# Streaming attention heads in tiles of 55 queries with all their 118 keys, in place of 96-key tiles

## The chip, the cores and the metric

One core of a Trainium2 chip. The metric is the device time of one execution in microseconds (us). Times are medians of the fast runs. A run is called slow when it lies over 1.5% above the fastest of the same kernel; slow runs are not used. Ratios are the mean time of one kernel's fast runs over that of the kernel before in the same rounds, so they are not quite the ratio of the medians quoted beside them. In the profiles PE is TensorE, ACT ScalarE, DVE VectorE, POOL GpSimd and SP SyncE; `[0.73 <-ACT ...]` says how long an engine stood still and what, as far as the profile can tell, ended the wait. The granted clock is the share of full speed that TensorE was given. PSUM is the memory that the matmuls here write. The kernel uses it in banks, and a matmul into a bank is made to wait for the engine that still reads it (in the kernel before, 0.35 us for ACT at 156.24 us).

## The reference, cut to what matters

Four batches of 8 attention heads over 768 positions, head size 64, then a mixture of four experts over all 3,072 rows. Three heads (0, 2, 6) see all earlier keys. Five heads (1, 3, 4, 5, 7) are streaming heads: each query sees the first 4 keys (the sinks) and the last 64.

```python
is_sink = pos[None, :] < 4
in_win = (rel >= 0) & (rel < 64)
stream_keep = causal & (is_sink | in_win)
scores = np.where(mask, scale * (q @ k.T), -1e9)
a = softmax(scores)                      # per row, with 1e-9 in the denominator
x = (a @ v) as rows of 8 * 64 = 512 columns
out = sum over e of p[:, e] * (relu(x @ w1[e]) @ w2[e])   # 512 -> 1024 -> 512
```

## The kernel before

The work goes in eight groups of 384 positions: batch b, half c (0 or 1). While TensorE runs the experts of group g, the attention of group g + 1 is woven in between as small steps, and GpSimd loads k, q and v for group g + 2. From batch 1 on, q and k go through staging tiles in row layout and are transposed by DMA. Scores stand with keys on the partitions, so a matmul takes one tile of keys as weights and the queries as its moving columns. Cuts are marked with `...`.

```python
TK = 96; R0 = P - TK; TQ = TK + NW            # a key tile: 96 keys, seen by up to 160 queries
kSr = [pers.tile([P, TC, NSH, P], FP16, ...) for c in range(NCH)]   # staging, one per half

def tiles_of(x, b, h, c):                     # 96 partitions, 4 tiles, 64 elements
    return x[b, h, c*CH:(c+1)*CH, :].rearrange("(t r) d -> r t d", r=TK)

def load_k(b, c):                             # fp32 in HBM -> fp16 in SBUF, issued by GpSimd
    for h in range(H):
        ...
        gp.dma_start(out=kSr[c][R0:P, :, SH.index(h), own(h)], in_=tiles_of(k, b, h, c))

def score_tiles(h):                           # streaming head: (key tile, column, first query, queries)
    if c == 0: return [(320, [(0, 0, 0, 160), (1, 160, 96, 160)], mask),
                       (256, [(2, 0, 192, 160), (3, 160, 288, 96)], mask)]
    return [(384, [(3, 0, 0, 64), (4, 64, 0, 160), (5, 224, 96, 160)], mask),
            (256, [(6, 0, 192, 160), (7, 160, 288, 96)], mask)]

def scores(h):                                # per score tile: matmuls, exp, mask
    for cols, parts, masks in score_tiles(h):
        ps = bank()                           # 4 PSUM banks, shared with the experts' first layer
        for n, (t, o, q0, nq) in enumerate(parts):
            nc.tensor.matmul(out=ps[:, o:o+nq], lhsT=key_tile(b, h, t), rhs=qTs[b, c][:, hp, q0:q0+nq], ...)
            ns += mm_ns(nq)                   # PE time as the kernel counts it, nq / 2.4 + 2.5 ns (384: 162.5; step in the trace 162)
        es = ...; nc.scalar.activation(out=es, in_=ps, func=AF.Exp, scale=SC)
        ... multiply by the mask on VectorE ...
        yield ns                              # values(h) yields likewise, then Ln and Exp on ScalarE

att_ns = 4500.0 if nxt % NCH == 0 else 7700.0 # total of the attention's ns for a half
for ns in moe_group(g):                       # weave by PE time spent
    spent += ns
    while done < (spent - begin) / (end - begin) * att_ns: done += next(att_steps)
```

The softmax here doesn't subtract the row's maximum and nothing guards it: scores larger than these inputs give would overflow.

## Time and profile before

| | before |
|---|---|
| median of 3 runs | 417.87 us (417.56 to 418.0) |
| span in the profile | 415.6 us |
| TensorE (PE) busy | 401.6 us, 97% |
| granted clock | 0.996 (1.00 from 68 to 415 us) |
| GpSimd's queue q0 | 71,872 packets |

The prediction below shows the lines of busy time, chain, matmuls and stalls. The records of matmuls overlap: one of 384 columns is recorded with 326 ns, and the next one starts 162 ns after it. So PE's stream is counted in steps from start to start. Two more lines, both of the first page of the kernel before: the share of time in which the DMA engines were busy, a digit of tenths for each of 40 slices (10.4 us each), and the packets, megabytes and share of the 16 engines' time of the GpSimd queue q0.

```profile
DMA  9999999999994700069963600046001000020002
...
q0 software_dynamic: 71872, 17.05, 45.8%
```

The engines are full until 125 us and then have long empty stretches.

### The profile page before, as it was taken

The numbers are of one execution on the slowest core, as the hardware profiler recorded it, in microseconds if no ns is written. First come the engines' busy times: TensorE is split into PE (matmuls) and PEld (weight loads), VectorE is DVE, ScalarE is ACT, GpSimd is POOL, SyncE is SP. The second block draws the span as 40 slices with busy tenths as digits, with TensorE's granted clock in tenths as the row PEclk, the third lists the DMA queues.
The fourth block names the chain that finished last, engine by engine and source line by source line (L and its number), as shares of the span: only waits on it lengthen the run. The fifth ranks groups of instructions, "written<-read, shape, count | busy, mean of one in ns | idle before, by whom it ended". The sixth has DMA issues, their size and how long they took to land.

```text
span 415.6 us, 6541 instructions
## 1 busy us (share of the span) xinstructions
PE 401.6 (97%) x2520; PEld 228.3 (55%) x2520; DVE 163.3 (39%) x332; ACT 249.3 (60%) x539; POOL 120.2 (29%) x176
## 2 busy tenths in 40 slices
PE   7899999999999999999999999999999999999996
PEld 4665554555555555555555555555555555555552
DVE  7976553224432335333433333234443233432222
ACT  2676874337775657666764558666665577653331
POOL 8938319897980000039930000000000000000000
PEclk9899999999999999999999999999999999999999
DMA  9999999999994700069963600046001000020002
GB/s 173 146 196 204 209 205 109 177 182 146 88 91 118 98 1 2 25 126 164 83 39 94 117 2 2 0 107 105 2 0 61 18 2 0 2 76 2 0 0 76
DMA packets 117554, 33.70 MB, mean 81 GB/s; under 512 B 108100, under 2 KB 112404, under 8 KB 117524
## 3 DMA queue, kind: packets, MB, share of 16 engines
q0 software_dynamic: 71872, 17.05, 45.8%
q1 hardware_dynamic: 42452, 15.46, 18.1%
q10 hardware_dynamic: 3200, 0.79, 0.9%
q8 instruction: 19, 0.31, 0.3%
q14 instruction: 11, 0.09, 0.1%
HBM read 35.70 MB, written 6.29 MB: 101 GB/s over the span
## 4 chain that ended last, share of the span: by engine, by line
PE 86%; ACT 6%; DVE 4%; issue 1%; DMA 1%; ACTq 0%; DVEq 0%
PE pO L669 39%; PE pA L648 35%; PE pV L529 5%; PE pA L481 5%; ACT hs L661 2%; ACT rc L548 2%; DVE kS L417 1%; DMA q<-in_q_dram 1%; DVE vS L218 1%; ACT es L499 1%; ACT rc L558 1%; DVE kR L401 1%; ACTq L279 0%; DVE qT L392 0%; DVE es L503 0%
## 5 line engine op out<-in xcount | busy, mean ns | idle before, releaser
L648 PE MATMUL pA<-xT,w1sb 128*128 128x384 f16 x1024 | 187.7, 326 | 1.5 <-DVE kS L417 1.0
L669 PE MATMUL pO<-w2sb,hs 128*128 128x512 f16 x768 | 180.7, 379 | 0.0
L661 ACT ACTIVATE hs<-pA 128x384 f16<-128x384 f32 x256 | 121.3, 493 | 80.0 <-PE pA L648 73.4
L648 PEld LDWEIGHTS <-w1sb 128*128 128x128 f16 x1024 | 97.3, 98 | 59.7 <-issue 1.8
L669 PEld LDWEIGHTS <-hs 128*128 128x128 f16 x768 | 72.8, 98 | 72.7 <-ACT hs L661 0.5
L499 ACT ACTIVATE es<-pA 128x256 f16<-128x256 f32 (+3 forms) x152 | 71.6, 481 | 32.5 <-PE pA L481 29.5
L685 DVE SCALAR_TENSOR_TENSOR acc<-pO,p_sb,acc 128x512 f32<-128x512 f32 x72 | 54.0, 750 | 85.3 <-PE pO L669 84.8
L503 DVE TENSOR_TENSOR es<-es,mS 128x384 f16<-128x384 f16 (+1 forms) x70 | 22.2, 317 | 85.4 <-ACT es L499 85.0
L548 ACT ACTIVATE rc<-pV,eps 64x384 f32<-64x384 f32 x60 | 34.5, 575 | 34.7 <-PE pV L529 33.9
L173 POOL DMA_DIRECT2D kSr<-in_k_dram x30 | 20.9, 700 | 54.9 <-DMA kSr<-kSr 42.1
L553 DVE TENSOR_TENSOR xT<-pV,rc 64x384 f16<-64x384 f32 x60 | 33.1, 552 | 4.1 <-PE pA L648 1.7
L681 DVE TENSOR_SCALAR acc<-pO,p_sb 128x512 f32<-128x512 f32 x24 | 18.0, 750 | 37.7 <-PE pO L669 36.8
L558 ACT ACTIVATE rc<-rc 64x384 f32<-64x384 f32 x58 | 30.2, 522 | 1.8
L211 POOL DMA_DIRECT2D vS<-in_v_dram x40 | 28.1, 706 | 2.9 <-DMA q<-in_q_dram 2.2
L481 PE MATMUL pA<-qT,kS 128*128 128x160 f16 (+2 forms) x180 | 23.7, 223 | 3.4 <-ACT es L499 1.8
L481 PE MATMUL pA<-qT,kR 128*128 128x384 f16 (+2 forms) x120 | 25.3, 281 | 0.0
L481 PEld LDWEIGHTS <-kS 128*128 128x128 f16 x180 | 15.9, 98 | 15.2 <-issue 4.5
L503 DVE TENSOR_TENSOR es<-es,mC 128x256 f16<-128x256 f16 (+1 forms) x42 | 10.8, 256 | 29.4 <-ACT es L499 29.0
L529 PE MATMUL pV<-es,vR 128*128 128x384 f16 (+2 forms) x120 | 21.9, 281 | 0.0
L169 POOL DMA_DIRECT2D kRr<-in_k_dram x18 | 13.5, 751 | 21.4 <-issue 17.1
L207 POOL DMA_DIRECT2D vR<-in_v_dram x24 | 18.2, 759 | 4.5 <-DMA w2sb<-in_moe_w_dram 4.2
L529 PEld LDWEIGHTS <-vS 128*128 128x128 f16 x180 | 13.7, 98 | 9.8 <-issue 2.2
(68 smaller groups left out, 153.0 us busy)
## 6 DMA issues: line engine op xcount, KB each, us to landing
out_dram<-acc SPq DMA_DIRECT2D x24, 256.0 KB
w1sb<-in_moe_w_dram POOLq DMA_DIRECT2D x4, 1024.0 KB, 14.6
w2sb<-in_moe_w_dram POOLq DMA_DIRECT2D x4, 1024.0 KB, 17.6
q<-in_q_dram POOLq DMA_DIRECT2D x18, 128.0 KB, 4.8
vS<-in_v_dram POOLq DMA_DIRECT2D x40, 48.0 KB, 3.3
kSr<-in_k_dram POOLq DMA_DIRECT2D x30, 48.0 KB, 4.5
vR<-in_v_dram POOLq DMA_DIRECT2D x24, 48.0 KB, 3.4
kRr<-in_k_dram POOLq DMA_DIRECT2D x18, 48.0 KB, 4.6
```

The costliest lines, as they stand in the source:

```text
L211: gp.dma_start(out=t[R0:P, TC * c : TC * (c + 1), own(h)], in_=tiles_of(v, b, h, c),)
L481: nc.tensor.matmul(out=ps[:, o : o + nq], lhsT=key_tile(b, h, t), rhs=qTs[b, c][:, hp, q0 : q0 + nq], start=(n == 0 or not first), stop=no ...
L499: nc.scalar.activation(out=es[:, 0:cols], in_=ps[:, 0:cols], func=AF.Exp, scale=SC)
L503: nc.vector.tensor_tensor(out=es[:, o0:o1], in0=es[:, o0:o1], in1=m[:, mo : mo + o1 - o0], op=ALU.mult,)
L529: nc.tensor.matmul(out=ps[:, q0 : q0 + nq], lhsT=v_tile(b, h)[:, t, :], rhs=es[:, o : o + nq], start=(n == 0), stop=(n == len(work) - 1), ...
L548: nc.scalar.activation(out=rc[r, :], in_=ps[o, 0:CH], func=AF.Ln, bias=eps[o, :])
L553: nc.vector.tensor_tensor(out=xT[g][r, hp, :], in0=ps[r, 0:CH], in1=rc[r, :], op=ALU.mult)
L558: nc.scalar.activation(out=rc[r, :], in_=rc[r, :], func=AF.Exp, scale=-1.0)
L648: nc.tensor.matmul(out=pss[ft][:, 0:CH], lhsT=w1sb[:, e * DMP + ct, ft * P : (ft + 1) * P], rhs=xT[g][:, ct, :], start=(ct == 0), stop=(ct ...
L661: nc.scalar.activation(out=hs[:, ft, :], in_=ps[:, 0:CH], func=AF.Relu)
L669: nc.tensor.matmul(out=ps_o, lhsT=hs[:, ft, j * P : (j + 1) * P], rhs=w2sb[:, e * FTP + ft, :], start=(ft == 0), stop=(ft == FTP - 1),)
L685: nc.vector.scalar_tensor_tensor(out=acc[nt], in0=ps_o, scalar=p_ap, in1=acc[nt], op0=ALU.mult, op1=ALU.add,)
```

## The change

The intent: cut the columns that PE streams for the streaming heads. A tile of 96 keys is streamed past 160 queries, though each query sees only 68 keys, so many queries pass two tiles. After the change a tile is 55 queries with every key that any of them sees: 55 + 63 = 118 consecutive keys, plus the 4 sinks, 122 of 128 partitions. Each query is then streamed exactly once. The price is that neighbouring tiles' keys overlap, so rows are loaded more than once.

```diff
+    WQ = 55
+    WK = WQ + NW - 1                      # 118
+    WT = 7
-    kSr = [pers.tile([P, TC, NSH, P], FP16, name=f"kSr{c}") for c in range(NCH)]
+    kSr = pers.tile([P, WT, NSH, P], FP16, name="kSr")       # one staging tile (kRr likewise)
+    def windows_of(x, b, h, c):
+        first = ((b * H + h) * S + c * CH - NW) * D
+        return bass.AP(x.tensor, x.offset + first, [[D, WK], [WQ * D, WT], [1, D]])
     ... load_k, load_v, batches 1 to 3 ...
-                    out=kSr[c][R0:P, :, SH.index(h), own(h)], in_=tiles_of(k, b, h, c)
+                    out=kSr[NS : NS + WK, :, SH.index(h), own(h)],
+                    in_=windows_of(k, b, h, c),
     ... score_tiles ...
+            if b:
+                starts = [max(WQ * t - 1, 0) for t in range(WT)] + [CH]
+                parts = [(t, q0, q0, q1 - q0) for t, (q0, q1) in enumerate(zip(starts, starts[1:]))]
+                return [(CH, parts, [(mWf, 1 + 2 * WQ * c, 0, CH)])]
-        att_ns = 4500.0 if nxt % NCH == 0 else 7700.0
+        att_ns = 3700.0 if nxt % NCH == 0 else 6600.0
```

Left out: the new mask mW, the copies of the sinks, and the sharing of buffers between batches. Batch 0 keeps the old tiles.

More of the change, by code (lines that the diff above doesn't have):

```diff
@@ L67 @@
     assert NS <= R0 and NW == 64 and NS + NW <= TK
+    WQ = 55
+    WK = WQ + NW - 1
+    WT = 7
+    assert WT * WQ - 1 == CH and NS + WK <= P
     pers = ctx.enter_context(tc.tile_pool(name="pers", bufs=1))
@@ L89, with windows @@
     kR = []
-    kS = []
+    kSf = []
     vR = []
-    vS = []
+    vSf = []
     for i in range(2):
         kR.append(pers.tile([P, NCH, NR, 3, P], FP16, name=f"kR{i}"))
-        kS.append(pers.tile([P, NCH, TC, NSH, P], FP16, name=f"kS{i}"))
+        kSf.append(pers.tile([P, NCH * TC * NSH * P], FP16, name=f"kS{i}"))
         vR.append(pers.tile([P, S // P, len(RH), P], FP16, name=f"vR{i}"))
-        vS.append(pers.tile([P, NT, len(SH), P], FP16, name=f"vS{i}"))
+        vSf.append(pers.tile([P, NT * NSH * P], FP16, name=f"vS{i}"))
+    kS = kSf[0].rearrange("p (c t s x) -> p c t s x", c=NCH, t=TC, s=NSH)
+    vS = vSf[0].rearrange("p (t s x) -> p t s x", t=NT, s=NSH)
+    def windows(x, c):
+        return x[1 - c][:, 0 : WT * NSH * P].rearrange(
+            "p (t s x) -> p t s x", t=WT, s=NSH
+        )
     ident32 = pers.tile([P, P], FP32, name="ident32")
@@ L106 @@
     mS = pers.tile([P, 4, TQ], FP16, name="mS")
+    mW = pers.tile([P, WT + 2, WQ], FP16, name="mW")
     probs = pers.tile([P, NTILE, E], FP32, name="probs")
@@ L110 @@
     p_sb = pers.tile([P, NTILE, E], FP32, name="p_sb")
-    kRr = [pers.tile([P, NR, 3, P], FP16, name=f"kRr{c}") for c in range(NCH)]
-    kSr = [pers.tile([P, TC, NSH, P], FP16, name=f"kSr{c}") for c in range(NCH)]
+    kRr = pers.tile([P, NR, 3, P], FP16, name="kRr")
+    kSr = pers.tile([P, WT, NSH, P], FP16, name="kSr")
     def own(h):
@@ L119, in own, with key_tile @@
         return slice(u * D, (u + 1) * D)
-    def key_tile(b, h, t):
+    def key_tile(b, c, h, t):
         i = b % 2
@@ L125, in key_tile, with v_tile @@
             return kR[i][:, t // 3, RH.index(h), t % 3, :]
-        return kS[i][:, t // TC, t % TC, SH.index(h), :]
-    def v_tile(b, h):
+        if b:
+            return windows(kSf, c)[:, t, SH.index(h), :]
+        return kS[:, t // TC, t % TC, SH.index(h), :]
+    def v_tile(b, c, h):
         i = b % 2
@@ L132, in v_tile @@
             return vR[i][:, :, RH.index(h), :]
-        return vS[i][:, :, SH.index(h), :]
+        if b:
+            return windows(vSf, c)[:, :, SH.index(h), :]
+        return vS[:, :, SH.index(h), :]
     q16 = {}
@@ L142, in tiles_of @@
         return x[b, h, c * CH : (c + 1) * CH, :].rearrange("(t r) d -> r t d", r=TK)
+    def windows_of(x, b, h, c):
+        assert b > 0
+        first = ((b * H + h) * S + c * CH - NW) * D
+        return bass.AP(x.tensor, x.offset + first, [[D, WK], [WQ * D, WT], [1, D]])
     def load_by_rows(x, x16, b, c):
@@ L169, in load_k @@
                 gp.dma_start(
-                    out=kRr[c][:, RH.index(h), :, own(h)], in_=rows_of(k, b, h, c)
+                    out=kRr[:, RH.index(h), :, own(h)], in_=rows_of(k, b, h, c)
                 )
@@ L183, in dma_transposes @@
         i = b % 2
-        first = kSr[0][R0 : R0 + NS, 0:1, :, :].rearrange("p t s x -> p t (s x)")
-        nc.sync.dma_start(
-            out=kSr[c][0:NS, :, :, :].rearrange("p t s x -> p t (s x)"),
-            in_=first.to_broadcast([NS, TC, NSH * P]),
-        )
+        if c == 0:
+            x = kSr.rearrange("p t s x -> p t (s x)")
+            nc.sync.dma_start(
+                out=x[0:NS, :, :],
+                in_=x[NS + NW : 2 * NS + NW, 0:1, :].to_broadcast([NS, WT, NSH * P]),
+            )
         alloc_qT(b, c)
@@ L195, in dma_transposes @@
             )
-        for x, xr in ((kR, kRr), (kS, kSr)):
+        for x, xr in ((kR[i][:, c, :, :, :], kRr), (windows(kSf, c), kSr)):
             nc.sync.dma_start(
-                out=x[i][:, c, :, :, :].rearrange("p t s x -> p (t s) x"),
-                in_=xr[c].rearrange("p t s x -> p (t s x)"),
+                out=x.rearrange("p t s x -> p (t s) x"),
+                in_=xr.rearrange("p t s x -> p (t s x)"),
                 transpose=True,
@@ L204, in load_v @@
         for h in heads:
-            t = v_tile(b, h)
+            t = v_tile(b, c, h)
             if RETR[h]:
@@ L208, in load_v @@
                     out=t[:, 3 * c : 3 * c + 3, own(h)], in_=rows_of(v, b, h, c)
+                )
+            elif b:
+                gp.dma_start(
+                    out=t[NS : NS + WK, :, own(h)], in_=windows_of(v, b, h, c)
                 )
@@ L216, in sink_row @@
     def sink_row(b, h, c):
-        t = v_tile(b, h)[:, :, own(h)]
+        t = v_tile(b, c, h)[:, :, own(h)]
         nc.vector.tensor_copy(
@@ L223, in sink_rows @@
     def sink_rows(b, c):
-        x = vS[b % 2].rearrange("p t s x -> p t (s x)")
-        nc.sync.dma_start(
-            out=x[0:NS, TC * c : TC * (c + 1), :],
-            in_=x[R0 : R0 + NS, 0:1, :].to_broadcast([NS, TC, NSH * P]),
-        )
+        x = vS.rearrange("p t s x -> p t (s x)")
+        to, src = x[0:NS, TC * c : TC * (c + 1), :], x[R0 : R0 + NS, 0:1, :]
+        if b:
+            to, x = (
+                windows(vSf, y).rearrange("p t s x -> p t (s x)") for y in (c, 0)
+            )
+            to = to[0:NS, :, :]
+            src = x[0:NS, 0:1, :] if c else x[NS + NW : 2 * NS + NW, 0:1, :]
+        nc.sync.dma_start(out=to, in_=src.to_broadcast(list(to.shape)))
     def load_w1(e, f0, f1):
@@ L260, in zero, with one_values_r, one_values @@
         fill(eng, t.rearrange("p a b x -> p (a b x)"), 0.0)
-    def one_values(eng, i, c):
+    def one_values_r(eng, i, c):
         t = slice(3 * c, 3 * c + 3)
         fill(eng, vR[i][:, t, :, D:P], ONES)
+    def one_values(eng, c):
+        one_values_r(eng, 0, c)
         t = slice(TC * c, TC * (c + 1))
-        fill(eng, vS[i][0:R0, t, :, :].rearrange("p t h x -> p t (h x)"), ONES)
-        fill(eng, vS[i][:, t, 0:2, 0:D], ONES)
-        fill(eng, vS[i][:, t, 2, D:P], ONES)
-        fill(eng, vS[i][:, t, 3:5, 0:D], ONES)
+        fill(eng, vS[0:R0, t, :, :].rearrange("p t h x -> p t (h x)"), ONES)
+        fill(eng, vS[:, t, 0:2, 0:D], ONES)
+        fill(eng, vS[:, t, 2, D:P], ONES)
+        fill(eng, vS[:, t, 3:5, 0:D], ONES)
     assert all(h % 2 == 0 for h in RH) and [h % 2 for h in SH] == [1, 1, 0, 1, 1]
@@ L294 @@
     make_identity(nc, ident32)
-    one_values(nc.vector, 0, 0)
+    one_values(nc.vector, 0)
     load_v(0, 0, [0, 1, 2, 3])
     zero(nc.vector, kR[0][:, 0, :, :, :])
-    zero(nc.vector, kS[0][:, 0, :, :, :])
+    zero(nc.vector, kS[:, 0, :, :, :])
     nc.vector.tensor_copy(out=ident16, in_=ident32)
@@ L339, in mask_s, with mask_w @@
         )
+    def mask_w():
+        gp.memset(mW, 1.0)
+        gp.affine_select(
+            out=mW, in_=mW, compare_op=ALU.is_ge, fill=0.0,
+            base=-NS, pattern=[[0, WT + 2], [-1, WQ]], channel_multiplier=1,
+        )
+        gp.affine_select(
+            out=mW, in_=mW, compare_op=ALU.is_ge, fill=0.0,
+            base=NS + NW - 1, pattern=[[0, WT + 2], [1, WQ]], channel_multiplier=-1,
+        )
+        for t in range(2):
+            gp.affine_select(
+                out=mW[:, t, :], in_=mW[:, t, :], compare_op=ALU.is_ge, fill=0.0,
+                base=WQ * t - NW - NS, pattern=[[0, WQ]], channel_multiplier=1,
+            )
+        gp.memset(mW[0:NS, 0, :], 0.0)
+        gp.memset(mW[0:NS, 1 : WT + 2, :], 1.0)
+        gp.affine_select(
+            out=mW[0:NS, 1, :], in_=mW[0:NS, 1, :], compare_op=ALU.is_ge, fill=0.0,
+            base=WQ - 1 - NW, pattern=[[1, WQ]], channel_multiplier=-1,
+        )
     mask_c(bC, 0.0, -60000.0)
@@ L350 @@
     zero(gp, kR[0][:, 1, :, :, :])
-    zero(gp, kS[0][:, 1, :, :, :])
-    one_values(gp, 0, 1)
+    zero(gp, kS[:, 1, :, :, :])
+    one_values(gp, 1)
     load_v(0, 1, range(5))
@@ L361 @@
     bSf = bS.rearrange("p t x -> p (t x)")
+    mWf = mW.rearrange("p t x -> p (t x)")
     xT = {}
@@ L410, in transposes @@
                     n = SH.index(h)
-                    x_in, x_out = ps[r, 0:CH], kS[i][r, c, :, n, R0:P]
+                    x_in, x_out = ps[r, 0:CH], kS[r, c, :, n, R0:P]
                     if first:
@@ L417, in transposes @@
                     nc.vector.tensor_copy(out=x_out, in_=x_in)
-                    sinks = kS[i][r, c, :, n, 0:NS]
+                    sinks = kS[r, c, :, n, 0:NS]
                     if c == 0:
@@ L450, in score_tiles @@
                 ]
+            if b:
+                starts = [max(WQ * t - 1, 0) for t in range(WT)] + [CH]
+                parts = [
+                    (t, q0, q0, q1 - q0)
+                    for t, (q0, q1) in enumerate(zip(starts, starts[1:]))
+                ]
+                return [(CH, parts, [(mWf, 1 + 2 * WQ * c, 0, CH)])]
             if c == 0:
@@ L482, in scores @@
                         out=ps[:, o : o + nq],
-                        lhsT=key_tile(b, h, t),
+                        lhsT=key_tile(b, c, h, t),
                         rhs=qTs[b, c][:, hp, q0 : q0 + nq],
@@ L530, in values @@
                     out=ps[:, q0 : q0 + nq],
-                    lhsT=v_tile(b, h)[:, t, :],
+                    lhsT=v_tile(b, c, h)[:, t, :],
                     rhs=es[:, o : o + nq],
@@ L696 @@
         pass
-    for c in range(NCH):
-        zero(gp, kRr[c])
-        zero(gp, kSr[c])
+    zero(gp, kRr)
+    zero(gp, kSr)
+    mask_w()
     UNIT = FTP * DMP * mm_ns(CH) + 3 * FTP * mm_ns(DM)
@@ L712 @@
             if b2 == 1:
-                one_values(gp, b2, c2)
+                one_values_r(gp, b2, c2)
+                fill(gp, windows(vSf, c2).rearrange("p t s x -> p (t s x)"), ONES)
             load_v(b2, c2, range(H))
@@ L717 @@
         end = {0: 2.2}.get(g, 0.93 * E) * UNIT
-        att_ns = 4500.0 if nxt % NCH == 0 else 7700.0
+        att_ns = 3700.0 if nxt % NCH == 0 else 6600.0
         if nxt < NCH:
-            att_ns += 8 * 3 * mm_ns(P)
+            att_ns += 1100.0 + 8 * 3 * mm_ns(P)
         spent = 0.0
```

## The prediction

> **What bounds the kernel now.** I read the first page first (busy time, slices, chain of waits), then the groups by shape, then the timeline of PE, then the waits, then the issues of the SP queue.
>
> ```profile
> PE 401.6 (97%) x2520; PEld 228.3 (55%) x2520; DVE 163.3 (39%) x332; ACT 249.3 (60%) x539; POOL 120.2 (29%) x176
> ...
> PE 86%; ACT 6%; DVE 4%; issue 1%; DMA 1%; ACTq 0%; DVEq 0%
> ...
> L648 PE MATMUL pA<-xT,w1sb 128*128 128x384 f16 x1024 | 187.7, 326 | 1.5 <-DVE kS L417 1.0
> L669 PE MATMUL pO<-w2sb,hs 128*128 128x512 f16 x768 | 180.7, 379 | 0.0
> ```
>
> PE is busy for 97% of 415.6 us, makes 86% of the chain that ended last, and its clock is granted in full. No other engine passes 60%. So PE is the bound, and what a change takes from its stream comes off the time, nearly one to one. [...] what a matmul takes from the stream is the step from its start to the next one's. The timeline of PE gives it:
>
> ```profile
> 33.96 0.81 PE L669 MATMUL pO<-w2sb,hs 128*128 128x512 f16 x3
> 34.60 0.33 PE L481 MATMUL pA<-qT,kS 128*128 128x64 f16 x3
> 34.77 0.33 PE L529 MATMUL pV<-es,vR 128*128 128x384 f16 x1
> ...
> 135.28 0.28 PE L481 MATMUL pA<-qT,kS 128*128 128x160 f16 x2
> 135.40 0.38 PE L669 MATMUL pO<-w2sb,hs 128*128 128x512 f16 x1
> ```
>
> The three at 34.60 (64+160+160 columns) last 0.17 us to the next start, the two at 135.28 (160+96) 0.12 us. That is columns/2.4 ns plus some 2 ns each: 29, 69 and 42 ns for 64, 160 and 96 columns. The 64-column one is the telling case: the weights of the matmul after it were loaded within its 29 ns, although the weight-load row (L481, kS) says 98 ns each.
>
> Where does PE stand still after the start-up? The step method finds 3.7 us of stalls from 68 us on, at two repeating places:
>
> ```profile
> 122.09 0.30 PE L529 MATMUL pV<-es,vS 128*128 128x160 f16 x2
> 122.62 0.27 PE L529 MATMUL pV<-es,vS 128*128 128x160 f16 x2 [0.23 <-DVE es L503]
> ...
> 155.07 0.81 PE L648 MATMUL pA<-xT,w1sb 128*128 128x384 f16 x4
> 156.24 0.33 PE L481 MATMUL pA<-qT,kS 128*128 128x64 f16 x3 [0.35 <-ACT hs L661]
> 156.62 0.81 PE L648 MATMUL pA<-xT,w1sb 128*128 128x384 f16 x4
> ```
>
> First place: 122.62 − 122.09 − 2 x 0.069 = 0.39 us. The last head's second score tile has just been issued and its values wait for exp and mask; it comes again at 218.2 and 314.7 (0.44 each), 1.27 us in all. Second place: 156.24 − 155.07 − 4 x 0.162 = 0.52, then 156.62 − 156.24 − 0.166 = 0.21: a streaming head's score tile waits for a PSUM bank that ACT has not yet emptied. It comes three times, 2.2 us. The other 0.2 us are small.
>
> [...]
>
> **The change, part by part.** It touches batches 1 to 3: 3 batches x 5 streaming heads = 15 head-passes for each half of the sequence (c = 0 and c = 1), each with scores and values.
>
> Columns: before, c = 0 streams 3 x 160 + 96 = 576 columns and c = 1 64 + 3 x 160 + 96 = 640, for scores and again for values. After, exactly 384 either way. Removed: 15 x 2 x (192 + 256) = 13,440 columns, at 2.4 per ns 5.6 us. (The instruction listing of both kernels gives 925,120 and 911,680 columns, the same difference.)
>
> Matmuls: 4 (c = 0) or 5 (c = 1) become 7. Added: 15 x 2 x (3 + 2) = 150. At columns/2.4 + 2 ns a 55-column matmul steps in 25 ns; the smallest step that the trace shows is 29. I take 26: 7 x 26 = 182 ns against 3 x 69 + 42 = 249 (c = 0) and 29 + 249 = 278 (c = 1). Gain 15 x 2 x (67 + 96) = 4.9 us. At 25 ns it is 5.3, at 29 ns 3.7.
>
> ACT and DVE: two exps and two masks per pass become one. Rows by shape: exp 434 + 383 ns (c = 0) and 493 + 383 (c = 1) become 493. ACT sheds 15 x (324 + 383) = 10.6 us of 249. The mask rows (225 ns for 128 columns, 290 for 256, 326 for 320, 358 for 384) rise by 0.52 ns a column[...]. Neither is on the path by itself; they count through the stalls. In the new order the last c = 0 head's values come after its only score tile with 16 layer-1 and 8 layer-2 matmuls in between (some 4.3 us; before, only 4 layer-2 matmuls stood there), so the first stall should vanish (−1.27). At the second, the bank holds one score tile a head, not two, and ACT has one exp fewer: I take two thirds of it away (−1.4) and add 0.4 for what appears elsewhere. Sum of stalls −2.3 us.
>
> DMA: each streaming head loads 118 x 7 = 826 rows of k and v in place of 384: 60 loads x 442 = 26,520 packets more in the GpSimd queue (71,872 now). The transposes of the streaming keys go from 20 to 35 blocks. The slices show DMA idle for much of the time from 140 us on, so this is hidden there. It is not idle early; see the first rival.
>
> Sum: 417.87 − 4.9 − 2.3 + 0.3 (the chance of the first rival times its cost) = 411.0 us.
>
> **Rivals.** A: the first attention by DMA (batch 1, c = 0) gets its keys too late.
>
> ```profile
> 65.80 0.64 SPq L185 DMA_DIRECT2D kSr<-kSr  x1
> 67.50 4.80 SPq L191 DMA_TRANSPOSE qT<-q  x3
> 72.39 1.92 SPq L197 DMA_TRANSPOSE kR<-kRr  x1
> 74.40 5.22 SPq L197 DMA_TRANSPOSE kS<-kSr  x1
> ...
> 93.98 0.30 PE L481 MATMUL pA<-qT,kS 128*128 128x160 f16 x2
> ```
>
> The loads are stuck behind the weights until 63 us, the copy of the sinks follows at 65.80, the last transpose is issued at 74.40 and its packets end near 81; the first streaming keys are used at 93.98. That leaves 13 us. After: the k loads land about 2 us later (2,210 more packets at some 1,000 a us)[...], and the transpose of 35 blocks lasts 6.6 x 1.75 = 11.5 us in place of 6.6. So it ends at 88 to 92. That still holds, with 2 to 6 us left. In addition there is now one staging buffer for keys, not two, so the next half's loads wait for this transpose; they are needed near 121 us, 30 us later. Chance of a stall some 12%, cost 2 to 4 us.
>
> B: short matmuls in a row do not step in 26 ns. Seven weight loads follow one another at 55 columns, and the trace has no two such short ones in a row. [...] Against it speaks the step of 29. A milder form, odd start columns (54, 109, ...) in the moving operand, is untested by this trace. Chance 6%.
>
> C: the stalls do not go. ACT and DVE work is spread by the same rule[...]. Then only columns count: 413.
>
> D: all the stalls go and the step is 25 ns: 417.87 − 5.3 − 3.7 = 408.9.
>
> **Range and chances.** The columns are sure to about 0.8 us either way, the stalls to about 1.5; A and B are tails on the slow side. So 408.8 to 414.4 for 8 in 10. Two per cent faster would be 409.5: that needs nearly D, 0.17. Two per cent slower needs B and A together, 0.02. The rest, 0.81, is within 2%.
>
> **What would show it.** Right, if in the profile after: PE has 2,670 matmuls; runs of seven 54/55-column ones take 0.17 to 0.19 us to the next start; no wait of the values for the mask at the ends of the c = 0 halves near 122, 218 and 314 us; ACT busy near 239; the GpSimd queue near 98,400 packets. [...] The first streaming scores of batch 1 start without idle time near 94 us. Wrong, if the seven take 0.3 us or more (B), if PE has a gap of over 1 us near 94 or 121 us (A), or if the waits of PE on ACT sum to as much as now (C).

## The result, and the profile after

| | before | after |
|---|---|---|
| median | 417.77 us (4 runs) | 608.1 us (4 runs, 607.06 to 609.9) |
| ratio, 95% interval | 1 | 1.456 (1.452 to 1.460) |
| PE busy | 401.6 us of 415.6 | 430.2 us of 605.4 |
| GpSimd busy | 120.2 us | 323.5 us |
| packets of q0 | 71,872 | 445,312 |

The kernel lost 190 us. These are lines of the first page of the kernel after: busy time, the DMA slices (15.1 us each now), q0, the chain that ended last by engine, and the costliest groups of GpSimd and of the new mask.

```profile
PE 430.2 (71%) x2670; PEld 232.7 (38%) x2670; DVE 154.3 (25%) x302; ACT 244.4 (40%) x509; POOL 323.5 (53%) x176
...
DMA  9999989999799987999879997799988999900001
...
q0 software_dynamic: 445312, 21.83, 80.0%
...
PE 28%; DMA 23%; issue 22%; POOL 22%; SPq 3%; ACT 1%; DVE 0%; POOLq 0%
...
L241 POOL DMA_DIRECT2D vS<-in_v_dram x30 | 120.4, 4014 | 129.5 <-issue 117.1
...
L200 POOL DMA_DIRECT2D kSr<-in_k_dram x30 | 120.2, 4008 | 58.1 <-issue 58.1
...
L576 DVE TENSOR_TENSOR es<-es,mW 128x384 f16<-128x384 f16 x30 | 10.8, 359 | 95.5 <-ACT es L572 95.4
```

PE is no longer the bound: 28% of the chain, against 86%. The chain now runs through DMA and through GpSimd's issue of loads. A load of streaming keys or values holds GpSimd for 4.0 us; before it was 0.7 (from the groups of the kernel before):

```profile
L173 POOL DMA_DIRECT2D kSr<-in_k_dram x30 | 20.9, 700 | 54.9 <-DMA kSr<-kSr 42.1 <-DMA w2sb<-in_moe_w_dram 8.1 <-DMA w1sb<-in_moe_w_dram 4.7
```

The DMA engines are busy until 530 us of 605. What PE waited for, from its view of waits (total us, times, longest):

```profile
PE pA L554 <- DMA kR<-kRr: 83.5, 6, 20.6
PE pV L602 <- DMA kSr<-in_k_dram: 44.9, 3, 16.0
PE pA L554 <- DMA kS<-kSr: 31.6, 6, 6.9
```

160 us of waits for keys and values that come late, in each of the six halves of batches 1 to 3. (The releaser in the second line is inferred; what the values need is the copy of the sinks, which waits for the loads.) With the waits the clock is lower as well: 0.861 of full speed on average against 0.996, 0.79 to 0.85 in the six stretches of 78 us from 63 to 531 us and 0.99 in the last 74 us, which have no such wait. The first two waits, in the timeline of PE:

```profile
110.61 0.61 PE L554 MATMUL pA<-qT,kR 128*128 128x128 f16 x2 [20.36 <-DMA kR<-kRr]
111.01 2.77 PE L721 MATMUL pA<-xT,w1sb 128*128 128x384 f16 x8
113.57 0.42 PE L554 MATMUL pA<-qT,kR 128*128 128x256 f16 x1
...
122.17 0.51 PE L554 MATMUL pA<-qT,kS 128*128 128x54 f16 x7 [6.90 <-DMA kS<-kSr]
```

After the first, eight matmuls of 384 columns take (113.57 − 111.01) / 8 = 0.32 us each; in the kernel before, at a granted clock of 1.00, it is 0.162 (23 of them from 71.76 to 75.49 us). The 160 us of waits and the 28.6 us by which PE is busy longer make up nearly all of the 189.8 us that the span grew. How late the loads are shows in the timeline of GpSimd, with the start and the length of each issue in us:

```profile
218.81 4.02 POOL L200 DMA_DIRECT2D kSr<-in_k_dram  x1 [1.58 <-issue]
225.67 3.98 POOL L200 DMA_DIRECT2D kSr<-in_k_dram  x1 [2.84 <-issue]
231.57 3.98 POOL L200 DMA_DIRECT2D kSr<-in_k_dram  x1 [1.93 <-issue]
237.95 4.02 POOL L200 DMA_DIRECT2D kSr<-in_k_dram  x1 [1.59 <-issue]
```

One load each 6.4 us, and GpSimd idles some 2 us before each: GpSimd's own work does not set the pace. Each of the four is issued 0.33 us after the load before last has landed (at 218.47, 225.33, 231.24 and 237.62 us by the trace's records of landings) and lands some 12 us later itself: two loads are in flight at a time, and never more than two of all 60. From the last weights' landing (63.6 us) to the last values' landing (531.1 us) the six halves take 467.6 us, 77.9 each (ten loads that land 5 to 7 us apart, but two or three of them, beside the transposes, 9 to 17), against the 48 us or so in which PE gets through a half. 63.6 + 467.6 + 74 us of work after the last landing is the span.

Why does a load of 826 rows take the queue 6.4 us? q0's packets tell how many packets it is. Before, each of the 60 streaming loads of batches 1 to 3 has 96 x 4 = 384 rows, one packet a row, and 16 packets of 4 bytes besides (in the packet records of the kernel before, q0 has 2,240 of 4 bytes: 16 for each of its 140 loads). So 71,872 - 60 x 400 = 47,872 packets belong to everything else. After: (445,312 - 47,872) / 60 = 6,624 a load, which is 16 x 413 + 16. And 413 = 59 x 7 is the number of rows on one engine when 118 partitions are shared by 2 engines. The packet records of the trace agree: 26,520 more packets of 128 bytes than before, just the predicted number, and 346,920 more of 4 bytes, which is 60 x 14 x 413. So two engines carry 413 rows each, and each of the other fourteen gets 413 packets of 4 bytes to go with them. (The records kept here do not name a packet's engine; the split is inferred from the counts, which it fits to the packet.)

What the small packets do is less certain than that they are there. They take time: of that of the 16 engines from 218.5 to 249.9 us, 44% went to packets of 4 bytes and 38% to those of 128. And they seem to take up places. With them two loads are 2 x 414 = 828 packets on each engine, and a third would make 1,242. Counted so, no GpSimd load of this kernel after 60 us is issued with more than 983 packets outstanding on an engine, itself included, and each issue that waited for a landing would have made it 1,023 or more. No run has few engines without the small packets, so how much of the loss is due to each stays open.

### The profile page after: what moved, and what is told of

Its sections match the earlier page's. It is cut to its first block, busy times and chain, and to the rows that moved or that the text cites. A ratio compares the mean times of both kernels' runs of the same rounds, so it can differ in the third digit from the quotient of the medians.

```text
span 605.4 us, 6780 instructions
## 1 busy us (share of the span) xinstructions
PE 430.2 (71%) x2670; PEld 232.7 (38%) x2670; DVE 154.3 (25%) x302; ACT 244.4 (40%) x509; POOL 323.5 (53%) x176
## 3 DMA queue, kind: packets, MB, share of 16 engines
q0 software_dynamic: 445312, 21.83, 80.0%
## 4 chain that ended last, share of the span: by engine, by line
PE 28%; DMA 23%; issue 22%; POOL 22%; SPq 3%; ACT 1%; DVE 0%; POOLq 0%
PE pA L721 13%; PE pO L742 12%; POOL kSr L200 9%; DMA kSr<-in_k_dram 7%; DMA kR<-kRr 6%; POOL vS L241 6%; DMA kS<-kSr 3%; DMA q<-in_q_dram 3%; DMA w1sb<-in_moe_w_dram 2%; SPq L221 2%; DMA k<-in_k_dram 2%; POOL kRr L196 2%; POOL vR L237 2%; PE pA L554 1%; PE pV L602 1%
## 5 line engine op out<-in xcount | busy, mean ns | idle before, releaser
L721 PE MATMUL pA<-xT,w1sb 128*128 128x384 f16 x1024 | 206.2, 349 | 3.9 <-ACT hs L734 2.5
L241 POOL DMA_DIRECT2D vS<-in_v_dram x30 | 120.4, 4014 | 129.5 <-issue 117.1
L742 PE MATMUL pO<-w2sb,hs 128*128 128x512 f16 x768 | 189.3, 392 | 0.0
L200 POOL DMA_DIRECT2D kSr<-in_k_dram x30 | 120.2, 4008 | 58.1 <-issue 58.1
L721 PEld LDWEIGHTS <-w1sb 128*128 128x128 f16 x1024 | 103.4, 104 | 76.2 <-issue 21.8
L572 ACT ACTIVATE es<-pA 128x512 f16<-128x512 f32 (+3 forms) x122 | 61.0, 510 | 140.6 <-PE pA L554 138.9
L554 PEld LDWEIGHTS <-kR 128*128 128x128 f16 x120 | 11.9, 105 | 96.5 <-DMA kR<-kRr 85.8
L602 PE MATMUL pV<-es,vS 128*128 128x55 f16 (+4 forms) x239 | 13.9, 196 | 47.1 <-DMA kSr<-in_k_dram 44.9
L554 PE MATMUL pA<-qT,kS 128*128 128x55 f16 (+4 forms) x255 | 17.4, 200 | 33.9 <-DMA kS<-kSr 31.6
L576 DVE TENSOR_TENSOR es<-es,mW 128x384 f16<-128x384 f16 x30 | 10.8, 359 | 95.5 <-ACT es L572 95.4
```

The source lines that it names most:

```text
L200: gp.dma_start(out=kSr[NS : NS + WK, :, SH.index(h), own(h)], in_=windows_of(k, b, h, c),)
L241: gp.dma_start(out=t[NS : NS + WK, :, own(h)], in_=windows_of(v, b, h, c))
L554: nc.tensor.matmul(out=ps[:, o : o + nq], lhsT=key_tile(b, c, h, t), rhs=qTs[b, c][:, hp, q0 : q0 + nq], start=(n == 0 or not first), stop ...
L572: nc.scalar.activation(out=es[:, 0:cols], in_=ps[:, 0:cols], func=AF.Exp, scale=SC)
L602: nc.tensor.matmul(out=ps[:, q0 : q0 + nq], lhsT=v_tile(b, c, h)[:, t, :], rhs=es[:, o : o + nq], start=(n == 0), stop=(n == len(work) - 1 ...
L721: nc.tensor.matmul(out=pss[ft][:, 0:CH], lhsT=w1sb[:, e * DMP + ct, ft * P : (ft + 1) * P], rhs=xT[g][:, ct, :], start=(ct == 0), stop=(ct ...
```

## The experiments

Theory A is this reading: the row count's largest divisor up to 16 sets how many DMA engines carry a GpSimd load, and all 16 are filled up to the same packet count. Its rivals: B, twice as many rows saturate the queue however they are split; C, the single staging tile chains loads behind transposes; D, the transposes of 35 blocks for 20 are at fault. Eight kernels were run. The first four (split112, before89, cuts, rows128) went to one chip together, the other four to another.

### split112: the same rows in two loads

```diff
+    ROWS = ((0, 112), (112, WK))
-                gp.dma_start(out=kSr[NS : NS + WK, ...], in_=windows_of(k, b, h, c))
+                for r0, r1 in ROWS:
+                    gp.dma_start(out=kSr[NS + r0 : NS + r1, ...], in_=windows_of(k, b, h, c, r0, r1))
     ... the same for v ...
```

> The changed kernel with each 118-row load issued as 112 rows and 6 rows; same rows, bytes, staging buffer, transposes and PE stream. Theory A (a GpSimd load spreads over as many DMA engines as the largest divisor up to 16 of its row count, and the other engines are filled up with as many 4-byte packets, so 118 rows cost 413 packets on each of 16 engines): 112 rows x 7 on 16 engines are 49 packets each and 6 x 7 on 6 engines 7 each, so the GpSimd queue falls from 445,312 packets to about 72,000 - 24,000 + 60 x (784 + 112 + 32) = 103,700, Pool's issue from 4.0 us to about 1.0 + 0.65, and the time to 411 us (409 to 414), as predicted for the columns. Theory B (the many more rows, 826 for 384, saturate the queue whatever their split): still over 550 us. Theory C (the single staging buffer orders loads behind transposes) and D (the transposes of 35 blocks): still over 500 us.

Correct. 414.89 us (five fast runs, 413.15 to 414.9), ratio 0.9935 (0.990 to 0.997). One run of six, the profiled one, was slow (466.71 us at a granted clock of 0.852) and is not used for time; its packet count stands:

```profile
q0 software_dynamic: 103552, 20.46, 53.1%
```

47,872 + 60 x (16 x 49 + 16 + 16 x 7 + 16) = 103,552, to the packet. Rows, bytes, staging tile, transposes and PE's order are those of the kernel after, and the 193 us are gone. B, C and D fall as causes of the loss. But 411 us, which I expected with the mechanism mended, was not reached; that is the second question, below.

### before89: one cause alone, in the kernel before

```diff
-                gp.dma_start(out=kSr[c][R0:P, ...], in_=tiles_of(k, b, h, c))
+                for r0, r1 in ((0, 89), (89, TK)):
+                    gp.dma_start(out=kSr[c][R0 + r0 : R0 + r1, ...], in_=tiles_of(k, b, h, c)[r0:r1])
     ... the same for v of batches 1 to 3 ...
```

> The kernel before, with nothing changed but that each 96-row load of streaming keys and values of batches 1 to 3 is issued as 89 rows and 7 rows. 89 is a prime. Theory A: one engine carries all 89 x 4 = 356 rows, the other 15 get 356 small packets each; 60 x (356 + 4 + 2) x 16 = 348,000 packets for these loads in place of 24,000; Pool 3.5 us a load, some 5.3 us of queue a load, 53 us a half against the 48 us that a half computes; time about 480 us (450 to 520). Theories B, C, D: the bytes, rows, buffers and transposes are those of before, so 418 us, plus at most 5 for the 60 more issues.

Correct. 537.51 us, ratio 1.291 (1.284 to 1.299). Nothing moved but where a load is cut: same bytes, rows, tiles and PE work as before. q0 has 395,392 packets, which is 47,872 + 60 x (16 x 356 + 16 + 16 x 4 + 16) exactly:

```profile
q0 software_dynamic: 395392, 18.34, 77.6%
```

The time lies above the 520 that I gave as its upper end: I had counted the queue alone, and loads beside the transposes land further apart (in this trace 9.6 us apart at 182.3 us, beside two transposes, and 5.3 at 209.2, beside none). That this is the whole of the excess was not tested.

### cuts: the rule of sizes

Each streaming head's 118 rows are cut elsewhere: 113+5, 116+2, 115+3, 117+1, 110+8.

> One look at the size rule: the changed kernel with its 118-row loads cut in another place for each head: 113+5, 116+2, 115+3, 117+1, 110+8. Theory A by divisors: 113 (prime) one engine, 791 packets on each; 116 four, 203; 115 five, 161; 117 thirteen, 63; 110 eleven, 70. Pool's issue at 0.6 us + 8.3 ns a packet: 7.2, 2.3, 1.9, 1.1 and 1.2 us. GpSimd queue packets 16 times the sum: 12 x 16 x (791+203+161+63+70 + 5 x 5) + 48,000 = about 300,000. Time about 470 us. Theory B: Pool's issue the same for all five within 10%, time as the changed kernel.

Correct, one look. GpSimd's issue of the large part of each load, from the views of the five lines (least, median and greatest ns; in the order 113, 116, 115, 117, 110 rows):

```profile
L210 POOL DMA_DIRECT2D kSr<-in_k_dram x6: 7192/7198/7202, 44.9 to 404.8; - x6
...
L213 POOL DMA_DIRECT2D kSr<-in_k_dram x6: 2301/2303/2303, 73.4 to 425.2; - x6
...
L216 POOL DMA_DIRECT2D kSr<-in_k_dram x6: 1911/1911/1920, 76.3 to 428.1; - x6
...
L219 POOL DMA_DIRECT2D kSr<-in_k_dram x6: 1079/1079/1097, 78.8 to 430.6; - x6
...
L222 POOL DMA_DIRECT2D kSr<-in_k_dram x6: 1186/1188/1197, 81.2 to 433.0; - x6
```

| rows | largest divisor up to 16 | packets on each engine (rows x 7 / divisor) | GpSimd's issue, us |
|---|---|---|---|
| 113 | 1 | 791 | 7.20 |
| 118 (kernel after) | 2 | 413 | 4.02 |
| 116 | 4 | 203 | 2.30 |
| 115 | 5 | 161 | 1.91 |
| 110 | 11 | 70 | 1.19 |
| 117 | 13 | 63 | 1.08 |
| 128 (rows128b) | 16 | 56 | 1.02 |

113 rows cost nearly seven times what 117 cost. The time follows packets per engine, with a slope of (7198 - 2303) / (791 - 203) = 8.3 ns a packet. q0 has 302,656 packets; the rule gives 47,872 + 12 x (16 x (791 + 203 + 161 + 63 + 70 + 29) + 160) = 302,656, where 29 is 7 + 7 + 7 + 1 + 7 for the small parts (5, 2, 3, 1 and 8 rows) and 160 are 16 packets of 4 bytes for each of ten loads. The kernel's own time, 551.67 us, was a miss (470 expected): the view of GpSimd's waits puts another 72 us before loads of values down to PE (the value tiles are still in use), which my sum over the queue did not have; this was not tested.

### rows128 and rows128b: one load of 128 rows

```diff
+    K0 = P - WK                                # the window at partitions 10 to 127
-        first = ((b * H + h) * S + c * CH - NW) * D
-        return bass.AP(x.tensor, x.offset + first, [[D, WK], ...])
+        first = ((b * H + h) * S + c * CH - NW - K0) * D
+        return bass.AP(x.tensor, x.offset + first, [[D, P], ...])
     ... the mask's NS becomes K0; the key sinks of half 0 are put aside in sinks_k for half 1 ...
     # rows128b adds:
+                src = sinks_v[0:NS, :, :]      # half 1; half 0 copies its value sinks there
```

> The changed kernel with one load of 128 rows a head (10 rows ahead of the window, masked or overwritten by the sinks), and a copy of the key sinks put aside for the second half. More bytes than the changed kernel, but 128 divides by 16. Theory A: 56 packets on each engine, 896 + 16 a load, Pool's issue about 0.9 us, time 411 us (409 to 414), equal to split112 within 1 us. Theories B, C, D: over 500 us, no better than the changed kernel.

rows128 gave a wrong result (relative error 0.12). By the program's order, the second half's copy of the value sinks is issued after the next batch's loads, and a 128-row load, unlike one of 118, overwrites those four rows, so the second half of batches 1 and 2 gets wrong sinks. That is a fault of my edit; its time, 414.54 us, has the same work in it. rows128b puts the value sinks aside.

> rows128 made correct: the value sinks of the first half are put aside too, since a 128-row load of the next batch overwrites them. PE's order, the loads and the transposes are those of rows128, plus one small copy per batch. Expected as rows128: ratio 0.993 to the kernel before (0.990 to 0.996), some 414.5 us, GpSimd queue 102,592 packets, and the same stalls of PE: 0.9 us between layer-1 matmuls near 157.7, 253.2 and 348.7 us.

Correct. 413.1 us (413.06 to 414.81), ratio 0.9922 (0.990 to 0.995), 102,592 packets as computed. More bytes than split112 (20.98 MB in q0 against 20.46), and no slower. The packets on each engine fell from 413 to 56, and the engines that carry rows rose from 2 to 16.

### Where the rest of the gain went: pace, pacehalf, beforepace

The mended kernels gain 3 to 4.5 us, not 7. The timeline of PE in rows128, whose profile is of a fast run, shows a place that comes back near 157.7 and 348.7 us:

```profile
248.45 0.81 PE L725 MATMUL pA<-xT,w1sb 128*128 128x384 f16 x4
249.10 0.36 PE L558 MATMUL pA<-qT,kS 128*128 128x54 f16 x7
249.30 0.81 PE L725 MATMUL pA<-xT,w1sb 128*128 128x384 f16 x4
249.95 0.36 PE L606 MATMUL pV<-es,vS 128*128 128x54 f16 x7
250.15 1.46 PE L725 MATMUL pA<-xT,w1sb 128*128 128x384 f16 x8
251.44 0.36 PE L558 MATMUL pA<-qT,kS 128*128 128x54 f16 x7
251.64 0.81 PE L725 MATMUL pA<-xT,w1sb 128*128 128x384 f16 x4
253.19 0.81 PE L725 MATMUL pA<-xT,w1sb 128*128 128x384 f16 x4 [0.73 <-ACT hs L738]
```

From 251.64 four matmuls need 0.65 us, so the next start should be 252.29; it is 253.19, a stall of 0.9 us, for a PSUM bank that ACT has not emptied. ACT at that time, same kernel:

```profile
249.06 0.58 ACT L625 ACTIVATE rc<-pV,eps 64x384 f32<-64x384 f32 x1
249.67 0.52 ACT L635 ACTIVATE rc<-rc 64x384 f32<-64x384 f32 x1
...
251.50 0.57 ACT L625 ACTIVATE rc<-pV,eps 64x384 f32<-64x384 f32 x1
252.10 0.52 ACT L635 ACTIVATE rc<-rc 64x384 f32<-64x384 f32 x1
252.65 0.87 ACT L738 ACTIVATE hs<-pA 128x384 f16<-128x384 f32 x2
```

The Ln and Exp of two neighbouring heads (1.1 us each) come 2.4 us apart. The weaving counts PE time: a streaming head's scores and values are cheaper for PE now, so I took their steps to come closer together, while each head's work on ACT after its values is what it was. At this very place that is not so. In the kernel before, the two are as close:

```profile
248.58 0.58 ACT L548 ACTIVATE rc<-pV,eps 64x384 f32<-64x384 f32 x1 [2.70 <-PE pV L529]
...
251.02 0.57 ACT L548 ACTIVATE rc<-pV,eps 64x384 f32<-64x384 f32 x1
```

and PE stalls there too, 0.74 us (the second place of the prediction). Over all of 68 us to the end it holds: 16 pairs of such Ln are under 3 us apart in rows128, 9 in the kernel before. Theory P: space the steps by PE and ACT together and these stalls go. Rival Q: ACT lacks room there whatever the order.

```diff
     # rows128b, steps of batches 1 to 3; w = 1 in pace, 0.3 in pacehalf
+                if b: ns += w * (0.83 * cols + 80.0)       # exp of a score tile
-            yield ns
+            yield ns + (w * 1100.0 if b else 0.0)          # Ln and Exp after a head's values
     ... att_ns is the sum of these over a half; beforepace: the same, w = 1, in the kernel before ...
```

> rows128b with the attention steps of batches 1 to 3 spaced by PE's and ACT's time together, not by PE's alone. Theory P (the 2.3 us of stalls that I expected to go stayed because shorter streaming matmuls bring the Ln and Exp of neighbouring heads, 1.1 us a head on ACT, closer together, so layer-1's banks are emptied late): the 0.9-us stalls go, PE's waits on ACT after 68 us fall from some 4.4 us to under 1.5, and the time falls 2.5 to 4 us below rows128b, to about 411. Rival Q (ACT has too little room in these stretches whatever the order): within 1 us of rows128b.

> As pace, with ACT's time weighted 0.3. Theory P: between rows128b and pace, or as pace if a little spacing is enough (411 to 413). Rival Q: as rows128b.

> The kernel before with the same spacing by PE and ACT and nothing else: what the spacing is worth without the change. Its stalls after 68 us are 3.7 us. If spacing takes most of them, 415 us (ratio 0.992 to 0.996); then the difference between pace and this run is what the 13,440 columns less are worth at the measured step of 28 ns, 3.8 us. If spacing does nothing here, 417.7.

| | median us | ratio to before (95%) | stalls of PE after 68 us |
|---|---|---|---|
| before | 417.61 | 1 | 3.7 |
| beforepace | 414.85 | 0.9949 (0.992 to 0.998) | 0.8 |
| rows128b | 413.1 | 0.9922 (0.990 to 0.995) | 5.2 |
| pace | 409.69 | 0.9827 (0.980 to 0.985) | none |
| pacehalf | 409.15 | 0.9814 (0.979 to 0.984) | 0.2 |

All correct. Stalls are start-to-start steps over what the columns need, of over 0.06 us, summed. P holds: the view of PE's waits after 68 us has this one line in rows128b and none at all in pace:

```profile
PE pA L730 <- ACT hs L743: 2.2, 3, 0.7
```

Both paced kernels beat rows128b and beforepace; over before they gain 1.7 to 1.9%. Two expectations were missed: pacehalf was to come to 411 to 413 and did as well as pace; and pace was to gain 3.8 us over beforepace and gained 5.2, of which 0.8 are stalls that beforepace keeps. The spacing also helps the kernel before (2.8 us), so the crowding is not of the change alone.

The sum closes for the two profiles. pace's profile has a span of 408.0 us and before's 415.6. Stalls give 3.7 us. The columns give 15 x 2 x (249 - 199 + 278 - 199) = 3.9 us, with the measured step of 28.4 ns for a 54/55-column matmul (7 x 28.4 = 199). 415.6 - 3.7 - 3.9 = 408.0. That it closes to 0.1 us is in part luck: runs of before had spans of 413.9, 415.6 and 417.4 us, all those of pace 408.0, and the ratio of the means gives 7.2 us, not 7.6.

## Why the prediction was wrong, point by point

**The step that failed is the DMA paragraph, and rival A that sized it.** It said that the added rows are "26,520 packets more in the GpSimd queue" and hidden after 140 us, and that the first keys land "about 2 us later". The 2 us count only packets that carry rows, at some 1,000 a us: the trace of the kernel before has q0 at 1,052 a us in its densest 5 us and at 776 in its densest 20. Of the 88 to 92 us at which the last transpose was to end, the 88 is worked out from the trace (81 + 2 + 4.9); the rest was my estimate, with loads on few engines running side by side, which no trace had shown. In fact the other fourteen engines are filled with as many 4-byte packets, and no more than two such loads were in flight: 373,440 packets more, 6.4 us a load and more beside the transposes, ten loads a half. That makes a half 77.9 us of loading against 48 of computing, six times over, where I had a single stall of 2 to 4 us at 12%. The sign that it named for A came true: gaps of 20.36 and 6.90 us in PE before the first keys of batch 1 are used. And for "two per cent slower" B was not needed: with this alone the kernel was 46% slower. The step was shown false by undoing it (split112, rows128b) and by doing it alone (before89), and its rule by cuts.

**Columns and matmuls:** 2,670 matmuls and 13,440 columns fewer, as said. The step is 28 ns (28.2 on average between 54/55-column matmuls in the last 74 us of the kernel after, 25 to 30 in rows128b), not 26: 3.9 us, not 4.9. The 64-column matmuls of the kernel before step in 28.3 ns on average, not 29, so the 54/55-column ones gain nothing over 64. Rival B, short matmuls that step more slowly in a row, did not occur: seven in a row step at 28 ns, 0.2 us in all, not 0.3.

**Stalls:** at the first place (values waiting for the mask at the end of a c = 0 half) they vanished, as said. At the second they did not fall by two thirds but rose, from 2.2 to 2.7 us in rows128, and others came up (0.56 us each near 143, 239 and 334 us), so that the sum of all went from 3.7 to 5.1 us. I had asked what ACT sheds and not when its work arrives. Rival C had this, with 413 us and no chance of its own; rows128b took 413.1. The predicted 411 is passed only with the steps respaced, which was no part of the predicted change.

**ACT and DVE:** ACT busy 241 us in rows128b (239 said). The mask took 359 ns for 384 columns: starting at an odd fp16 column cost nothing, in both halves (columns 1 and 111), against 358 ns for the old mask at an even one in the kernel before. I had expected it to be slower for its odd start column, an estimate of mine that no trace had shown.

**The rest of rival A:** the single staging tile and the longer transposes cost PE no wait once the loads are short: after 68 us, rows128b has none on DMA.

## What to carry to other kernels

Before changing a tile's size, factor its partition count: here, with seven pieces a partition, a GpSimd load of 113, 116 or 118 partitions put 791, 203 or 413 packets on all 16 engines, where 112 or 128 put 49 or 56. Round up to a multiple of 16 and mask the surplus, or cut the load there. All of these loads turn fp32 into fp16 on the way; no plain copy, and none of another queue, was tried. And when a change makes steps cheaper on the engine that is the bound, look at what each step hands to the next engine: work woven by one engine's clock can bunch on another.

## What else the traces show

- The rule of the largest divisor held for 89, 110, 113, 115, 116, 117 and 118 rows of GpSimd loads: q0's packets come out to the packet (395,392 in before89, 302,656 in cuts, 445,312 in the kernel after). The other engines get as many 4-byte packets (14 x 413 a load in the kernel after); at most two such loads were in flight.
- GpSimd's issue grew by some 8.4 ns for each packet per engine, from 0.7 us (24 packets, kernel before) to 7.2 us (791, cuts).
- With a weight load before each matmul, 54, 55 and 64 columns all step at 28 ns; 128 columns step at 56 ns in the kernel before.
- A tensor_tensor whose second fp16 operand starts 2 bytes off took 359 ns for 384 columns (kernel after), as one at an even column did (358 ns, kernel before).
- Fast runs of one kernel fall on levels some 1.7 us apart (before: 415.9, 417.7 and 419.4 us). In the profiles of rows128 and rows128b the first 40 us alone differ by 1.7 us. The cause was not looked into.
